# Two experts of the first batch move from the direct first stage to the Strassen-like slots of the second

## The chip, the cores and the metric

The program runs on one core of one Trainium2 chip, as one launch. The metric is the device time of the execution in microseconds (us). Beside it, a hardware profiler takes one execution apart into the instructions of each engine: TensorE (PE, with its weight loads as PEld), VectorE (DVE), ScalarE (ACT), GpSimd (POOL) and SyncE (SP), which here issues the DMAs. Each engine works through its own instructions strictly in the order written, and waits on semaphores for what other engines and DMAs produce.

## The reference, cut to what matters

```python
attn = clustered_attention(q, k, v, centroids)      # 4 batches, 8 heads, 768 rows, head size 64
x = attn.transpose(0, 2, 1, 3).reshape(3072, 512)
logits = x @ w_gate                                 # 8 experts
P = exp(logits - logits.max())
for _ in range(8):                                  # balanced over tokens and experts
    P /= P.sum(1, keepdims=True) + 1e-9
    P /= P.sum(0, keepdims=True) + 1e-9
    P *= N / E
for e in range(8):                                  # w1: 512 x 1024, w2: 1024 x 512
    out += P[:, e:e+1] * (relu(x @ w1[e]) @ w2[e])
```

All 3072 tokens go through all 8 experts.

## The kernel before, in words

The kernel has three parts one after the other: attention for all batches (to about 477 us of the span), a **first stage** that puts batch 0 through the 8 experts (to about 955 us), and a **second stage** that puts batches 1 to 3 through them (to the end). Every fp32 operand of a product is held as a sum of two fp16 halves, a high and a low one, and a product is three matmul passes (high by high, high by low, low by high).

**First layer, both stages.** `layer1` computes relu(x @ w1) for one quarter of an expert (256 of the 1024 hidden columns) with seven block products instead of eight (Strassen's method in Winograd's form). Each product is 6 matmuls of 384 columns (line 1387). It needs seven forms of the weights (three plain blocks and the sums S1 to S4) and seven of x. The results go through two PSUM banks in turn (`h_tile`): a quarter takes a bank for its first, second and fifth product, so that the first and the second product of a quarter can only begin when the sixth and the seventh of the quarter before have been read out by VectorE (`add`, line 1401).

**First stage.** The loop over t = 0 to 31 (lines 1582 to 1649) takes one quarter of an expert per turn of the loop, t = 4 * expert + quarter. In each of the seven products m of quarter t the program writes, in this order: the product and its read-out (`step(one)`), VectorE's low halves of relu results (`rests`), a piece of the magnitude scan for a later quarter (`scanning`), a piece of preparing x of batch 1 (`inputs`), a piece of making the weights for quarter t+1 (`making`), and one sixth of the second layer of quarter t-1 (`before`). This order is fixed on each engine by `plan.keep_order`. The second layer here is done directly: 36 matmuls of 512 columns per quarter (lines 1547 to 1549) into six PSUM banks, which collect over the four quarters of an expert. After an expert's last quarter VectorE multiplies the six banks by the gate and adds them to `acc` (lines 1560 and 1562), one per product of the following quarter.

Weights come raw from HBM (`load_raw`, 1 MB per quarter, 7 quarters ahead). ScalarE takes their magnitudes (`scan`, `total`, line 298), from which a power of two per expert is spread over all partitions by two small DMAs (`spread_powers`). `make_w` (lines 1507 to 1530) then makes the fp16 forms: ScalarE scales and makes high halves (1512, 1516, 1522, 1499), GpSimd the four sums and the low halves of w1's forms (332, 1517, 1524), VectorE the low halves of w2 (1502). `store_w` writes them to HBM, since the second stage uses them again. The forms of w1 live in a pool of three buffers (`wap`).

In quarters 1 to 3 the 8 rounds of balancing the gates (`gates`, lines 1289 to 1320) run on VectorE. Each round ends in a small matmul that rides in a product of those quarters (line 1315), the next round begins with its result.

**Second stage.** 24 slots, one per batch and expert. In slot n the first layer of (batch, expert) n runs with the second layer of slot n-1, 28 pairs of a first-layer product (6 matmuls of 384 columns) and a piece of the second layer (9 matmuls of 256 columns, line 1805). Here the second layer too is done with seven products, so it is 252 matmuls of 256 columns per expert. The hidden blocks are combined on GpSimd (`minus`, 1681), split by ScalarE and VectorE (1696, 1700), and the results are collected in four tiles C11, C21, C12, C22 and X by `evict` (1776, 1778). In the first eight slots the sums of w2 that this form needs are also made and stored (`second_sums`, `second_high`, `second_low`, lines 1706 to 1724).

The change touches the loop of the first stage, `load_raw`, `first_matrix`, `store_w`, `gated`, the pools at lines 1457 to 1465, the list of slots, `plan_slot`, `evict`, `layer1b` and `layer2b`.

Of the kernel before, what the change touches and what calls it, by code (L numbers as in the profile page):

```python
# [8 lines left out]
F32 = mybir.dt.float32  # L9
# [13 lines left out]
P = 128  # L23
# [141 lines left out]
def attn_moe_kernel(  # L165
# [138 lines left out]
    NP2 = NF // 2  # L304
    NI = E * NP2
# [977 lines left out]

    def h_tile():
        return ps_h.tile([P, 512], F32, name="h_ps")
# [36 lines left out]
    def spread_powers(am, n, name, use):  # L1322
# [4 lines left out]
        t = gs.tile([P, P, n], F32, name=f"all{n}", bufs=1)  # L1327
# [127 lines left out]
    before = iter(())  # L1455

    with ExitStack() as ax:
# [6 lines left out]
        accp = pool("accp", 1, ax)  # L1464
# [3 lines left out]
        def load_raw(idx):  # L1468
            e, f2 = divmod(idx, NP2)
            fs = slice(f2 * 2 * P, (f2 + 1) * 2 * P)  # L1470
            t = rawp.tile([P, 2048], F32, name="raw")
            nc.sync.dma_start(out=t[:, 0:1024].rearrange("p (c f) -> p c f", c=NC), in_=w1[e, :, fs].rearrange("(c p) f -> p c f", p=P))
            nc.sync.dma_start(out=t[:, 1024:2048].rearrange("p (j m) -> p j m", j=2), in_=w2[e, fs, :].rearrange("(j p) m -> p j m", p=P))
            raws[idx] = t
# [17 lines left out]
        def first_matrix(idx):  # L1492
            raw = raws[idx][:, 0:1024]
            return raw, raw.rearrange("p (k c t f) -> p t k c f", k=2, c=KC, t=2), sump.tile([P, 4, KC, P], F32, name="s1w")
# [37 lines left out]
        def store_w(idx, wt):  # L1532
            e, f2 = divmod(idx, NP2)
            wa, wb = wt
            if idx > 1:
                nc.sync.dma_start(out=w1d[idx], in_=wa.rearrange("p x a c f -> p (x a c f)"))
# [17 lines left out]
        def gated(e, acc):  # L1554
            gates_ = gate_values(0, e)

            def done(i, ps):
                gate = gates_[:, i : i + 1]
                if e == 0:
                    nc.vector.tensor_scalar(out=acc[:, i], in0=ps, scalar1=gate, scalar2=None, op0=ALU.mult)  # L1560
                else:
                    nc.vector.scalar_tensor_tensor(out=acc[:, i], in0=ps, scalar=gate, in1=acc[:, i], op0=ALU.mult, op1=ALU.add)
                if e == E - 1 and i % 2 == 1:
                    nc.scalar.dma_start(out=out_v[0][:, i - 1 : i + 1], in_=acc[:, i - 1 : i + 1])
# [3 lines left out]
        AHEAD = 7  # L1568
# [9 lines left out]
        acc = accp.tile([P, NT, DO], F32, name="acc")  # L1578
        scans = {i - 5: (i,) for i in range(8, NI)}
        loads = {0: (), 1: (4, 5), 2: (6, 7, 8), 3: (9, 10)}  # L1580
        loaded = {}
        for t in range(NI):
# [3 lines left out]
            for idx in loads.get(t, (t + AHEAD,) if t + AHEAD < NI else ()):  # L1586
                load_raw(idx)
            if 0 < t < NI - 1:
# [316 lines left out]
```

## Time and profile before

| | us |
|---|---|
| median of 3 runs | 2281.86 (2281.69 to 2282.4) |
| the profiled execution's own time | 2279.16 |
| its span, first to last instruction | 2277.1 |
| TensorE busy | 2236.1 (98%) |
| VectorE busy | 1649.1 (72%) |
| ScalarE busy | 1143.1 (50%) |
| GpSimd busy | 1118.1 (49%) |
| granted TensorE clock, mean | 0.995 |

The page in 40 slices of 57 us each (a digit is the busy share of a slice in tenths). The first stage is from the 9th to the 17th digit, the second stage follows:

```profile
PE   6999999999999999999999999999999999999999
DVE  7988878567666766588788877776676666666667
ACT  7777786555666665354444443333433333333333
POOL 3676787854555655276666653233332332322223
DMA  5345453365555543586766765544444554434433
```

Two things have to be kept in mind with such rows. Matmuls are pipelined, and one that shows 326 ns of duration follows the one before after about 163 ns, so the distance between starts is the measure. And the idle time of an engine that is not on the chain costs nothing.

### The profile page before, as it was taken

The numbers are of one execution on the slowest core, as the hardware profiler recorded it, in microseconds if no ns is written. First come the engines' busy times: TensorE is split into PE (matmuls) and PEld (weight loads), VectorE is DVE, ScalarE is ACT, GpSimd is POOL, SyncE is SP. The second block draws the span as 40 slices with busy tenths as digits, with TensorE's granted clock in tenths as the row PEclk, the third lists the DMA queues.
The fourth block names the chain that finished last, engine by engine and source line by source line (L and its number), as shares of the span: only waits on it lengthen the run. The fifth ranks groups of instructions, "written<-read, shape, count | busy, mean of one in ns | idle before, by whom it ended". The sixth has DMA issues, their size and how long they took to land.

```text
span 2277.1 us, 39662 instructions
## 1 busy us (share of the span) xinstructions
PE 2236.1 (98%) x15491; PEld 1458.8 (64%) x15491; DVE 1649.1 (72%) x2777; ACT 1143.1 (50%) x2107; POOL 1118.1 (49%) x997
## 2 busy tenths in 40 slices
PE   6999999999999999999999999999999999999999
PEld 3455554445555555567777777777777777777777
DVE  7988878567666766588788877776676666666667
ACT  7777786555666665354444443333433333333333
POOL 3676787854555655276666653233332332322223
PEclk7999999999999999999999999999999999999999
DMA  5345453365555543586766765544444554434433
GB/s 128 88 101 159 103 142 98 124 218 198 186 168 190 190 139 111 203 300 210 223 218 218 239 219 169 176 144 132 151 156 141 182 170 139 131 130 132 138 130 102
DMA packets 226860, 369.78 MB, mean 162 GB/s; under 512 B 73800, under 2 KB 163824, under 8 KB 226160
## 3 DMA queue, kind: packets, MB, share of 16 engines
q1 hardware_dynamic: 226240, 365.67, 50.3%
q8 instruction: 121, 1.98, 0.4%
q10 hardware_dynamic: 432, 1.57, 0.2%
q14 instruction: 67, 0.55, 0.1%
HBM read 272.22 MB, written 80.62 MB: 155 GB/s over the span
## 4 chain that ended last, share of the span: by engine, by line
PE 91%; DVE 6%; ACT 2%; issue 1%; DMA 1%; SPq 0%; DVEq 0%; ACTq 0%
PE h_ps L1387 38%; PE pb L1805 12%; PE pa L1805 8%; PE pc L1805 8%; PE av_ps L1004 4%; PE o_ps L1547 4%; PE o_ps L1549 4%; PE o_ps L1548 4%; PE exp_ps L945 2%; PE max_ps L849 2%; PE exp_ps L946 2%; DVE mrt L853 2%; PE misc_ps L1045 1%; PE misc_ps L630 1%; ACT pe L952 0%
## 5 line engine op out<-in xcount | busy, mean ns | idle before, releaser
L1387 PEld LDWEIGHTS <-wa 128*128 128x128 f16 x5376 | 525.6, 98 | 302.8 <-issue 5.3
L1805 PEld LDWEIGHTS <-ho 128*128 128x128 f16 x5940 | 580.8, 98 | 137.2 <-DVE ho L1700 1.1
L1387 PE MATMUL h_ps<-xsT,wa 128*128 128x384 f16 x3072 | 581.6, 326 | 1.2 <-DVE xsT L324 0.6
L1387 PE MATMUL h_ps<-xsB,wa 128*128 128x384 f16 x2304 | 436.9, 326 | 1.4 <-DVE B L1401 0.6
L1681 POOL TENSOR_TENSOR B<-B,B 128x768 f32<-128x768 f32 x96 | 197.9, 2064 | 468.2 <-DVE ho L1700 426.6
L1700 DVE TENSOR_TENSOR ho<-B,ho 128x768 f16<-128x768 f32 x283 | 348.1, 1230 | 1.6 <-ACT ho L1696 1.6
L1851 ACT ACTIVATE B<-B 128x384 f32<-128x384 f32 x288 | 149.7, 520 | 371.3 <-DVE B L1401 370.0
L1805 PE MATMUL pb<-w2o,ho 128*128 128x256 f16 x2532 | 322.2, 273 | 0.0
L1401 DVE SCALAR_TENSOR_TENSOR u<-h_ps,m 128x384 f32<-128x384 f32 x256 | 141.7, 553 | 243.5 <-PE h_ps L1387 240.7
L1696 ACT CAST ho<-B 128x768 f16<-128x768 f32 x283 | 226.8, 824 | 14.1 <-POOL B L1681 13.4
L970 POOL TENSOR_TENSOR psum<-psum,pe 128x512 f32<-128x512 f32 x160 | 208.1, 1317 | 43.6 <-ACT pe L952 40.3
L853 DVE TENSOR_REDUCE mrt<-max_ps 128x1 f32<-128x512 f32 (+1 forms) x288 | 188.8, 683 | 41.0 <-PE max_ps L849 39.7
L1805 PE MATMUL pc<-w2o,ho 128*128 128x256 f16 x1692 | 215.7, 273 | 0.3
L1805 PE MATMUL pa<-w2o,ho 128*128 128x256 f16 x1692 | 215.1, 273 | 0.0
L1681 POOL TENSOR_TENSOR B<-B,T 128x768 f32<-128x768 f32 x48 | 95.6, 1991 | 206.0 <-DVE ho L1700 206.0
L952 ACT ACTIVATE pe<-exp_ps 128x512 f32<-128x512 f32 x288 | 164.8, 597 | 56.9 <-PE exp_ps L946 51.2
L1411 ACT ACTIVATE m<-h_ps 128x384 f32<-128x384 f32 x128 | 62.6, 489 | 191.6 <-PE h_ps L1387 190.8
L1849 ACT ACTIVATE B<-h_ps 128x384 f32<-128x384 f32 x96 | 47.1, 490 | 211.4 <-PE h_ps L1387 211.4
L1549 PE MATMUL o_ps<-wb,hl 128*128 128x512 f16 x384 | 145.5, 379 | 0.0
L1548 PE MATMUL o_ps<-wb,hh 128*128 128x512 f16 x384 | 145.5, 379 | 0.0
L1547 PE MATMUL o_ps<-wb,hh 128*128 128x512 f16 x384 | 145.5, 379 | 0.0
L1610 ACT ACTIVATE hh<-c 128x384 f16<-128x384 f32 x128 | 66.9, 523 | 143.2 <-DVE c L1401 142.0
(281 smaller groups left out, 3280.8 us busy)
## 6 DMA issues: line engine op xcount, KB each, us to landing
wa<-w1d SPq DMA_DIRECT2D x98, 896.0 KB
w2o<-w2d SPq DMA_DIRECT2D x168, 512.0 KB
raw<-in_moe_w SPq DMA_DIRECT2D x60, 512.0 KB
w1d<-wa SPq DMA_DIRECT2D x30, 896.0 KB
r<-in_moe_w SPq DMA_DIRECT2D x32, 512.0 KB
w2d<-w2s SPq DMA_DIRECT2D x32, 512.0 KB
w2d<-wb SPq DMA_DIRECT2D x96, 128.0 KB
scan<-in_moe_w SPq DMA_DIRECT2D x32, 256.0 KB
```

The lines of the kernel that those rows point to most:

```text
L853: nc.vector.tensor_reduce(out=t["mr"][:, i0 : i0 + ni, ni - 1], in_=ps.rearrange("p (x c) -> p x c", x=ni), axis=AX, op=ALU.max)
L952: nc.scalar.activation(pe, ps.rearrange("p (x c) -> p x c", x=ni), AF.Exp, scale=SCALE)
L970: (nc.gpsimd if e == POOL else nc.vector).tensor_tensor(out=st[:, o : o + N0], in0=old[o], in1=part, op=ALU.add)
L1387: nc.tensor.matmul(ps[:, 0:HB], wa[:, w_, a, c, :], x[:, x_, c, :], start=(first and s_ == 0), stop=(s_ == len(steps) - 1), skip_group_che ...
L1547: nc.tensor.matmul(po[i], hh[:, t, ti], wbh[:, t], start=(first and t == 0), stop=False)
L1548: nc.tensor.matmul(po[i], hh[:, t, ti], wbl[:, t], start=False, stop=False)
L1549: nc.tensor.matmul(po[i], hl[:, t, ti], wbh[:, t], start=False, stop=(last and t == 1))
L1681: nc.gpsimd.tensor_tensor(out=t, in0=d[a], in1=d[c], op=ALU.subtract)
L1696: nc.scalar.copy(t[:, 0], blocks[n, g][o])
L1700: nc.vector.tensor_tensor(out=t[:, 1], in0=blocks[n, g][o], in1=t[:, 0], op=ALU.subtract)
L1805: nc.tensor.matmul(ps[q], h[:, h_, f, q * P : (q + 1) * P], w[:, 2 * g + f, w_], start=(first and g == 0 and s_ == 0 and q % 2 == 0), stop ...
L1851: rests.append(lambda: nc.scalar.activation(c, c, AF.Relu))
```

## The change

Experts 6 and 7 of batch 0 no longer go through the first stage. They become the first two slots of the second stage, which then has 26 slots; the loop of the first stage ends after 24 quarters (`NB`).

- Their weights were made by `make_w` in quarters 23 to 30. Now a generator `later` makes them during quarters 1 to 23, one turn per product (turn k falls in quarter 1 + k // 7, product k % 7 counted from 0). From turn 4 to turn 35 it takes the magnitudes of the 16 raw halves, one every second turn, alternately on ScalarE (`total`, w1) and on VectorE (`largest`, w2). From turn 36 a fixed list makes one quarter's weights every 13 turns, mostly one piece per turn. The raw halves are loaded twice, once for each purpose, into a pool of three half-size buffers.
- In that list the four sums are made on VectorE, where `make_w` has them on GpSimd. The low halves of the w1 forms stay on GpSimd.
- The fp16 forms use the same three buffers of `wap` as the quarters of the loop; they are stored to HBM by turn 16 of each quarter's list.
- Raw loads of the loop run 6 quarters ahead instead of 7, and the pool of raw tiles has 6 buffers instead of 8.
- The first stage's results are collected in the tiles C11, C21, C12, C22 of the second stage instead of `acc`: two evictions of 256 columns per bank instead of one of 512. X begins in the first slot. The output of batch 0 is written in the second slot, as that of the other batches in their last one.
- x of batch 1 is reloaded in the second slot instead of in the last quarter of the first stage.
- The w2 sums are made in the first eight slots of the new list, so for experts 6 and 7 first.

```diff
+    STD = E - 2
...
-        wbp = pool("wbp", 3, ax)
+        wbp = pool("wbp", 4, ax)
+        NB = STD * NP2
-        rawp = pool("rawp", 8, ax)
+        rawp = pool("rawp", 6, ax)
...
         def store_w(idx, wt):
+            if idx > 1:
+                store_first(idx, wt[0])
+            store_second(idx, wt[1])
...
             def done(i, ps):
                 gate = gates_[:, i : i + 1]
+                j, q = divmod(i, 3)
+                for r, name in enumerate((("C11", "C21"), ("C12", "C22"))[j]):
+                    o, y = totals[name][:, q], ps[:, r * HD : (r + 1) * HD]
+                    if e == 0:
+                        nc.vector.tensor_scalar(out=o, in0=y, scalar1=gate, scalar2=None, op0=ALU.mult)
+                    else:
+                        nc.vector.scalar_tensor_tensor(out=o, in0=y, scalar=gate, in1=o, op0=ALU.mult, op1=ALU.add)
...
-        AHEAD = 7
+        AHEAD = 6
...
+        def later():
+            whole = [(e, f2, m) for e in range(STD, E) for f2 in range(NP2) for m in range(2)]
+            todo, ahead, spreads = whole + whole, [], []
+            def fetch():
+                if todo:
+                    e, f2, m = todo.pop(0)
+                    t = rawp.tile([P, 1024], F32, name="rawx", bufs=3)
+                    fill_half(t, e, f2, m)
+                    ahead.append(t)
...
+            for _ in range(3):
+                fetch()
+            yield from wait(4)
+            for e in range(STD, E):
+                am = gs.tile([P, 2, NP2], F32, name="am8x")
+                for f2 in range(NP2):
+                    for m in range(2):
+                        t = ahead.pop(0)
+                        if m:
+                            largest(am[:, m, f2 : f2 + 1], t)
+                        else:
+                            total(am[:, m, f2 : f2 + 1], t, junkp.tile([P, 1024], F16, name="junk"))
+                        yield from wait(1)
+                        fetch()
+                        yield from wait(1)
+                am2 = gs.tile([P, 2], F32, name="am2x")
+                nc.vector.tensor_reduce(out=am2, in_=am, axis=AX, op=ALU.max)
+                spreads.append(spread_powers(am2, 2, f"amw{e}", lambda g, e=e: weight_use(e, g, gs), "x"))
...
+                return {
+                    0: [lambda: nc.scalar.activation(t1, t1, AF.Copy, scale=s1[:, e : e + 1])],
+                    2: [lambda: summed(0, 1)],
+                    3: [second_high],
+                    4: [lambda: summed(2, 3)],
+                    5: [plain_high],
+                    6: [lambda: second_low(0)],
+                    7: [lambda: plain_low(0)],
+                    8: [lambda: second_low(1), lambda: nc.scalar.copy(into["wa"][:, 0, 3:7], S_)],
+                    9: [lambda: plain_low(1)],
+                    11: [lambda: sum_low(0), fetch],
+                    12: [lambda: store_second(idx, into["wb"])],
+                    13: [lambda: sum_low(2), fetch],
+                    16: [lambda: store_first(idx, into["wa"])],
+                }
+            TURN = 13
...
+        extra = later()
-        for t in range(NI):
+        for t in range(NB):
...
                 if m:
                     step(making)
+                if t > 0:
+                    step(extra)
                 if m:
                     step(before)
                 if m == 1:
                     store_w(t, wt)
-                if t == NI - 1:
-                    reload_x(1, RIGHT[m])
...
-    slots = [(b, e) for b in range(1, B) for e in range(E)]
+    slots = [(0, e) for e in range(STD, E)] + [(b, e) for b in range(1, B) for e in range(E)]
...
-        if b == 1:
+        if n < E:
```

## Rows read from the trace of the kernel before

**Rows 1.** The page's first part: busy us, share of span, instructions

```profile
PE 2236.1 (98%) x15491; PEld 1458.8 (64%) x15491; DVE 1649.1 (72%) x2777; ACT 1143.1 (50%) x2107; POOL 1118.1 (49%) x997
```

**Rows 2.** The page's chain that ended last, shares of the span by line

```profile
PE h_ps L1387 38%; PE pb L1805 12%; PE pa L1805 8%; PE pc L1805 8%; PE av_ps L1004 4%; PE o_ps L1547 4%; PE o_ps L1549 4%; PE o_ps L1548 4%; PE exp_ps L945 2%; PE max_ps L849 2%; PE exp_ps L946 2%; DVE mrt L853 2%; PE misc_ps L1045 1%; PE misc_ps L630 1%; ACT pe L952 0%
```

**Rows 3.** Chain in order of time, first stage: start us, us, what

```profile
903.64 1.95 PE h_ps L1387 x12
918.24 1.95 PE h_ps L1387 x12
```

**Rows 4.** The same view, one slot of the second stage apart

```profile
1697.32 0.97 PE h_ps L1387 x6
...
1752.13 0.97 PE h_ps L1387 x6
```

**Rows 5.** The same view, start of the first stage

```profile
512.01 0.51 DVE csum L1312
512.56 0.39 PE h_ps L1315 x2
```

**Rows 6.** VectorE's timeline there: start us, us, instruction, idle before

```profile
508.10 0.75 DVE L1502 SCALAR_TENSOR_TENSOR wb<-raw,s,wb 128x512 f16<-128x512 f32 x1
509.09 0.17 DVE L1318 TENSOR_SCALAR csum<-h_ps 128x8 f32<-128x8 f32 x1 [0.25 <-ACT m L1411]
523.31 0.55 DVE L1401 SCALAR_TENSOR_TENSOR c<-h_ps,u 128x384 f32<-128x384 f32 x1
535.24 0.56 DVE L1401 SCALAR_TENSOR_TENSOR c<-h_ps,m 128x384 f32<-128x384 f32 x1 [0.99 <-PE h_ps L1387]
```

**Rows 7.** TensorE at the second product of two quarters, timeline

```profile
524.43 1.14 PE L1387 MATMUL h_ps<-xsT,wa 128*128 128x384 f16 x6
...
729.32 1.14 PE L1387 MATMUL h_ps<-xsT,wa 128*128 128x384 f16 x6
```

**Rows 8.** Timeline of VectorE, quarter after an expert's end

```profile
726.33 1.64 DVE L1502 SCALAR_TENSOR_TENSOR wb<-raw,s,wb 128x512 f16<-128x512 f32 x1
727.89 0.74 DVE L1562 SCALAR_TENSOR_TENSOR acc<-o_ps,gates,acc 128x512 f32<-128x512 f32 x1
728.55 0.54 DVE L1401 SCALAR_TENSOR_TENSOR c<-h_ps,u 128x384 f32<-128x384 f32 x1
```

**Rows 9.** Stretches: us; busy PE, PEld, DVE, ACT, POOL; clock; DMA share, GB/s

```profile
510.00:520.00 10.00, 9.24 (x52) 4.88 (x51) 9.36 (x24) 4.43 (x8) 5.14 (x7) 1.00 1.07 385
713.80:728.40 14.60, 14.60 (x80) 7.64 (x79) 11.72 (x18) 9.81 (x16) 8.09 (x8) 1.00 0.56 191
```

**Rows 10.** VectorE's reductions to one column by line: ns min/median/max

```profile
L301 DVE TENSOR_REDUCE am<-xqB x12: 936/944/949, 609.6 to 1483.1; 128x1 f32<-128x768 f32 x12
L301 DVE TENSOR_REDUCE amx<-xT x1: 3333/3333/3333, 178.8 to 178.8; 128x1 f32<-128x3072 f32 x1
```

**Rows 11.** VectorE's only sums of line 332, 128 wide

```profile
L332 DVE TENSOR_TENSOR tx<-tx x4: 271/282/293, 303.5 to 444.5; 128x128 f32<-128x128 f32 x4
```

**Rows 12.** Groups by line of the whole span: an eviction of the second stage

```profile
L1778 DVE SCALAR_TENSOR_TENSOR C<-pb,gates,C 128x256 f32<-128x256 f32 x204 | 86.0, 476 | 19.4 <-PE pb L1805 19.4
```

**Rows 13.** Groups by line, ACT, steady first stage: busy us, mean ns

```profile
L298 ACT ACTIVATE junk<-raw 128x1024 f16<-128x1024 f32 x46 | 48.0, 1044 | 0.0
L1512 ACT ACTIVATE raw<-raw,s 128x1024 f32<-128x1024 f32 x27 | 30.8, 1139 | 10.0 <-DVE s L267 10.0
L1522 ACT CAST wa<-s1w 128x1024 f16<-128x1024 f32 x27 | 27.8, 1028 | 0.0
```

**Rows 14.** Groups by line, POOL, the same stretch

```profile
L1524 POOL TENSOR_TENSOR wa<-s1w,wa 128x512 f16<-128x512 f32 x54 | 70.3, 1323 | 53.2 <-ACT wa L1522 53.2
L1517 POOL TENSOR_TENSOR wa<-raw,wa 128x512 f16<-128x512 f32 x27 | 36.9, 1367 | 0.0
```

**Rows 15.** SyncE's waits in the first stage: total us, times, longest

```profile
SPq L1328 <- DMA amw<-am: 15.0, 6, 2.9
```

**Rows 16.** The chain in order of time, start of the second stage

```profile
983.12 2.24 DVE ho L1700
```

More of the change, by code (lines that the diff above doesn't have):

```diff
@@ L1320, in gates, with spread_powers @@
             nc.vector.tensor_tensor(out=pr, in0=pr, in1=c2.unsqueeze(1).broadcast_to([P, NTT, E]), op=ALU.mult)
-    def spread_powers(am, n, name, use):
+    def spread_powers(am, n, name, use, own=""):
         d = dram.tile([P, n], F32, name=name)
@@ L1326, in spread_powers @@
         yield
-        t = gs.tile([P, P, n], F32, name=f"all{n}", bufs=1)
+        t = gs.tile([P, P, n], F32, name=f"all{n}{own}", bufs=1)
         nc.sync.dma_start(out=t, in_=d.partition_broadcast(P))
@@ L1455, in attn_moe_kernel, with total_tile @@
     before = iter(())
+    totals = {}
+    def total_tile(name):
+        return accp.tile([P, 3, HD], F32, name=name, bufs=2 if name == "C21" else 1)
     with ExitStack() as ax:
@@ L1493, in first_matrix @@
             raw = raws[idx][:, 0:1024]
-            return raw, raw.rearrange("p (k c t f) -> p t k c f", k=2, c=KC, t=2), sump.tile([P, 4, KC, P], F32, name="s1w")
+            return raw, raw.rearrange("p (k c t f) -> p t k c f", k=2, c=KC, t=2), sump.tile([P, 4, KC, P], F32, name="s1w" if idx < NB else "s1x")
         def second_matrix(idx, wb):
@@ L1581, in attn_moe_kernel, with enumerate_quarter @@
+        def enumerate_quarter(i, idx, turn):
+            return [(i * turn + y * 1, (i, y)) for y in (0, 2, 3, 4, 5, 6, 7, 8, 9, 11, 12, 13, 16)]
+        extra = later()
+        for name in ("C11", "C21", "C12", "C22"):
+            totals[name] = total_tile(name)
+        loads = {0: (), 1: (4, 5), 2: (6, 7, 8), 3: (9,)}
         loaded = {}
-        for t in range(NI):
+        for t in range(NB):
             e, f2 = divmod(t, NP2)
@@ L1585, in attn_moe_kernel @@
                 po = []
-            for idx in loads.get(t, (t + AHEAD,) if t + AHEAD < NI else ()):
+            for idx in loads.get(t, (t + AHEAD,) if t + AHEAD < NB else ()):
                 load_raw(idx)
-            if 0 < t < NI - 1:
+            if 0 < t < NB - 1:
                 wts[t + 1] = w_tiles()
                 making = make_w(t + 1, wts[t + 1])
-            if t + 2 >= NI:
+            if t + 2 >= NB:
                 loaded[t + 2] = load_wa((t + 2) % NI)
@@ L1648, in attn_moe_kernel @@
             wts.pop(t - 1, None)
-            before = layer2(po, hh, hl, wt, f2 == 0, f2 == NP2 - 1, gated(e, acc) if f2 == NP2 - 1 else None)
-        for x in (sink, inputs, scanning):
+            before = layer2(po, hh, hl, wt, f2 == 0, f2 == NP2 - 1, gated(e) if f2 == NP2 - 1 else None)
+        for x in (sink, inputs, scanning, extra):
             for _ in x:
@@ L1773, in evict @@
                 t, gate = totals[name][:, q], gates_[:, 3 * j + q : 3 * j + q + 1]
-                if e == 0 and (name, q) not in begun:
+                if (e == 0 or n == 0 and name == "X") and (name, q) not in begun:
                     begun.add((name, q))
@@ L1797, in layer2b @@
                 if name not in totals:
-                    totals[name] = accp.tile([P, 3, HD], F32, name=name, bufs=2 if name == "C21" else 1)
+                    totals[name] = total_tile(name)
             count = 0
```

92 lines of the change are left out of this document (68 added, 24 removed).

## The prediction

> **What bounds the kernel now.** I read the busy shares first: TensorE is at work for 98% of the span, the next engine for 72% [rows 1]. The chain that ended last confirms it: nearly all its shares are TensorE lines, 38% of them the first layer's [rows 2]. So a change pays by taking matmul time away, and loses where another engine makes TensorE wait. Then I looked for the pace in both stages. In the chain, the pair of products that begins a quarter of the first stage starts at 903.64 and again at 918.24, so a quarter takes 14.60 us [rows 3], and an expert 4 x 14.60 = 58.40. In the second stage the same place of a slot comes 54.81 us later [rows 4]. All quarters from the fifth on and nearly all slots keep these paces, so there is hardly a wait in either to be won. The third reading is the exception, the start of the first stage: there the chain runs through VectorE. TensorE waits for the end of a round of the gates (512.01 + 0.51, matmul at 512.56) [rows 5], and VectorE is busy 9.36 of 10 us in that stretch [rows 9].
>
> **What the change removes and adds on TensorE.** Two experts leave the first stage (2 x 58.40 = 116.80) and come back as two slots (2 x 54.81 = 109.62): 7.18 us less. Nothing else changes on TensorE's own list. The slots in which w2's sums are made are still eight, so the two new ones are slots without this work.
>
> **What it adds elsewhere.** The weights of the eight late quarters were made in the eight quarters that are now gone; they are made now beside 23 others. I go through the engines by what TensorE would wait for.
>
> *VectorE, magnitudes.* Eight reductions of 1024 columns. The trace has 768 columns in 0.944 us and 3072 in 3.333 [rows 10], so (3.333 - 0.944) / 2304 = 1.037 ns a column, and 1024 take 1.21 us. They come at turns 6, 10, 14, 18 (quarters 1 to 3, the stretch where VectorE has no room) and 22, 26, 30, 34.
> - Turn 6 stands behind the low half that ends at 508.10 + 0.75 = 508.85; the next round of the gates begins at 509.09 after 0.25 us of idle time [rows 6]. Of 1.21 us, 0.96 push the round, and TensorE already waits for its end: +0.96.
> - Turn 10 pushes the last read-out of quarter 2 from 523.31 to 524.52, with its 0.55 to 525.07 [rows 6]. That read-out frees the bank of the next quarter's second product, which starts at 524.43 [rows 7]: +0.7 with the hand-over.
> - Turns 14 and 18 stand among the last rounds. The first idle time behind them is 0.99 at 535.24 [rows 6]; of 2.42 us some 1.4 are left and a part falls into quarter 4: I take +1.2.
> - Turn 26 falls into the sixth product of quarter 4, where expert 0 is evicted. The pattern is that of quarter 16: low half, eviction, then the last read-out at 728.55 to 729.09 [rows 8], and the bank is wanted at 729.32 [rows 7]. Only 0.23 us are free, so of 1.21 us about 1.0, with the longer eviction ahead (below) 1.2. Turns 22, 30 and 34 fall where VectorE waits for TensorE anyway: nothing.
>
> Together 0.96 + 0.7 + 1.2 + 1.2 = 4.1. The ends: 0.96 if only the first is felt, five times 1.21 = 6.1 if all five are felt in full.
>
> *VectorE, evictions.* A bank took one eviction of 0.74 [rows 8], it takes two of 256 columns now, 0.476 each by the second stage's row [rows 12]: 0.21 more per bank. Five of six have TensorE's end of the bank behind them, the one ahead of the last read-out uses up the 0.23 us of slack named above. I take nothing for it alone; if that slack is less than it looks, 5 x 0.21 = 1.05.
>
> *VectorE, sums and low halves.* Each quarter of the list has four sums and two low halves. The sums on VectorE are not in this trace at 256 columns: at 128 they take 0.282 [rows 11], so up to 0.56 by twice that, and at least 0.28. A low half is the same instruction as in `make_w`, 0.75 alone and 1.64 beside GpSimd [rows 6, 8]. In a quarter with evictions VectorE is busy 11.72 of 14.60 us [rows 9]; 2.2 us come on top in the mean (2 x 0.56 a turn twice, and 2 x 1.2, in 13 turns of 2.1 us, makes 4.6 per 27 us). It fits, but the slack is not everywhere. In quarters 8, 12 and 16 such a pair or half falls into the fifth product, just ahead of the tight place of [rows 8]. The idle time there takes most of it: I take 0.4 each, 1.2 in all; between 0 and 3 x 1.64 = 4.9. In other quarters the last read-out has no evictions ahead, nothing.
>
> *ScalarE.* Magnitudes 1.04, scaling 1.14, high halves about 1.03 to 1.14 by the same rows [rows 13], one piece a turn of 2.1 us. ScalarE is busy 9.81 of 14.60 us in a full quarter [rows 9] and some 2 us come on top; it has most of a product to spare before TensorE needs the bank that it reads. Nothing; if the cover is gone it is the second rival.
>
> *GpSimd.* Two low pieces of 1.32, one of 1.37 and one of about half of that per 13 turns [rows 14], on an engine that is busy 8.09 of 14.60 [rows 9]: nothing for itself. But it does its work beside VectorE. The row shows what that costs VectorE: the low half 1.64 instead of 0.75 [rows 6, 8]. The Trainium skill, SBUF — State Buffer, "Who interferes with whom", says why: a VectorE instruction with two SBUF inputs and a GpSimd instruction that reads SBUF exclude each other, and the later one waits for the whole of the other; the two rows agree with it. What this could make of the time stands under the third rival.
>
> *DMA and SP.* 16 MB of halves are read (twice 8 MB), where 8 MB were read raw. At the start the queues run at 385 GB/s with a share of 1.07, so they are full [rows 9]. Three halves of 0.5 MB ahead of the loads cost 1.6 MB / 385 = 4 us of queue, and each half is fetched five turns (over 10 us) before use: I take nothing. Upper end: one such wait of 4 us.
>
> *Border of the stages.* The start of the second stage keeps its waits on VectorE, 2.24 us on the chain [rows 16], with less DMA beside it, since x is reloaded a slot later. Nothing; between -2.24 and, at the new border of batches, +2.24.
>
> **Sum.** -7.18 + 4.1 + 1.2 = -1.9 us. The profiled execution took 2279.16 us, so 2277.3 by its own time; the median of the runs is 2.7 above it, and the same difference makes 2281.86 - 1.9 = **2280.0**. What the measurement can tell from no change is 0.2%, 4.6 us.
>
> **Rivals.**
>
> 1. *VectorE recovers.* If its backlog at the start is worked off in the gaps, only turn 6 is felt, and -7.18 + 0.96 = -6.2: 2275.7. For it: TensorE waits for VectorE only where a bank or a round is due, and the fixed list puts single pieces between. Against it: the row of 9.36 in 10 us, and the 0.23 us of slack.
>
> 2. *The third weight buffer is the wait (slower).* The list takes its fp16 tile at its turn 5 from the same three buffers as the loop. With two tiles of the loop in between, it gets the buffer of the list's quarter before, whose store is issued at that quarter's turn 16, two turns (4.3 us) before ScalarE wants to write. The store is 0.9 MB: 2.4 us at 385 GB/s, and a small DMA on this queue is waited for 2.9 us at the longest [rows 15], so 5.3 us. When SP issues the store no earlier than its turn, ScalarE stands for a microsecond seven times and more where SP is held up, and behind it stand the read-outs that TensorE needs. With 1.2 us each reaching TensorE: 7 x 1.2 = 8.4 on top of -1.9, +6.5: 2288.4. It decides from 0.95 us each. Against it: SP may issue as soon as GpSimd's last low piece is done, at turn 14.
>
> 3. *VectorE and GpSimd block each other.* The list moves pieces to both. If in each of the 16 quarters with the list (turns 36 to 143, quarters 6 to 21) half of the 0.89 us (1.64 - 0.75) reaches the last read-out: 16 x 0.45 = 7.2 on top, +5.3: 2287.2. The rule of the skill named above would work in this way. Against it: GpSimd and VectorE overlap in every quarter now, and no quarter from the fifth on loses anything.
>
> 4. *The gain isn't there:* a slot at the head of the second stage could be slower than 54.81. The rows of both kinds of slots speak against it.
>
> **How the numbers follow.** The forecast has 0.52, rival 1 0.26, rivals 2 and 3 together 0.20, rival 4 0.02 with no gain left. The unknown costs alone reach from 7.18 - 0.96 = 6.2 below (8.5 if the border's 2.24 go as well) to 6.1 + 1.05 + 4.9 - 7.18 = 4.9 above, with one DMA wait 8.9 above. I take 2275.6 to 2287.0; what lies above is the worse half of rivals 2 and 3. By the 4.6 us: faster 0.26, no change 0.54, slower 0.20. The forecast's own range is 2277.5 to 2284.
>
> **What would show it.** Quarters of 14.60 us and slots of 54.81 with 26 of them: the gain. First stage: quarters 1 to 4 longer by 3 to 5 us together, with TensorE waiting on VectorE (rounds and read-outs), and quarters 9, 13 and 17 beginning with a wait of a few tenths. If ScalarE's first copy into the list's tile waits for a DMA, rival 2 is at work; if quarters without evictions grow too while VectorE's low halves take 1.6 us throughout, rival 3. I am wrong if quarters 1 to 4 keep their length, or if the waits come from a queue that I priced at nothing.

## The result, and the profile after

The changed kernel took 2307.76 us (median of 4 runs, 2304.91 to 2310.28) against 2282.13 for the kernel before on the same chip: ratio 1.011 with a 95% interval of 1.0094 to 1.0126. It is 25.6 us slower. Forecast were 2280.0, in a range up to 2287.0: the prediction was wrong. Each profile is of one execution: that of the kernel before took 2279.16 us, that of the changed kernel 2304.91.

The page of the changed kernel, its busy shares and the shares of the chain that ended last:

```profile
span 2303.1 us, 40251 instructions
...
PE 2239.4 (97%) x15707; PEld 1481.5 (64%) x15707; DVE 1706.7 (74%) x2885; ACT 1148.2 (50%) x2111; POOL 1137.2 (49%) x983
...
PE 80%; DVE 10%; DMA 4%; ACT 2%; POOL 2%; issue 1%; SPq 1%; DVEq 0%; ACTq 0%; POOLq 0%
```

The last of these lines in the page of the kernel before:

```profile
PE 91%; DVE 6%; ACT 2%; issue 1%; DMA 1%; SPq 0%; DVEq 0%; ACTq 0%
```

TensorE's share of the chain fell from 91% to 80%; VectorE, DMAs and GpSimd took its place. Where that is shows in the length of each quarter, which I take from the start of a quarter's first product to that of the next (every 42nd matmul of line 1387, after the change 1390). Quarters 0 to 22, in us. (The last quarter of the loop, 31 before and 23 after, takes 22.4 us both times: it holds the border of the stages, 7.8 us.)

| quarters | before | after |
|---|---|---|
| 0 to 3 | 14.65 15.33 16.04 15.29 | 16.07 15.34 16.87 16.84 |
| 4 to 7 | 14.60 each | 21.62 14.60 17.62 16.52 |
| 8 to 11 | 14.60 each | 14.60 16.54 14.60 17.12 |
| 12 to 15 | 14.60 each | 16.57 15.39 14.91 16.00 |
| 16 to 22 | 14.60 each | 16.74 15.26 15.71 15.82 16.23 14.74 14.60 |

The sum closes. From the last quarter's end to the end of the span the second stage takes 1431.6 us instead of 1322.1: 109.5 more, which is two slots of 54.8 [rows 4]. Eight quarters of 14.60 are gone (116.8), so 7.3 us are won. The 24 quarters left, the border among them, are 31.7 longer than the same ones before, and the stage begins 1.6 later: -7.3 + 31.7 + 1.6 = 26.0, the difference of the spans.

The largest single loss is quarter 4. The chain of the changed kernel, start and length in us:

```profile
545.66 4.84 DMA amw<-am2x
550.51 5.16 DMA all2x<-amw
555.69 0.43 DVE gmax L1335
...
557.87 0.48 DVE u L1404
558.39 2.08 PE h_ps L1390 x6
```

These are the two small DMAs that spread the magnitude of expert 6. The list put the reduction of `all2x` three turns (6.3 us) behind `am2x`; the DMAs took 10 us, and VectorE, which works in order, stood at the reduction. Behind it stood the evictions and the read-out `u` that TensorE needs. In VectorE's timeline (idle time before, and what ended it, in brackets):

```profile
555.69 0.42 DVE L1335 TENSOR_REDUCE gmax<-all2x 128x2 f32<-128x256 f32 x1 [6.79 <-DMA all2x<-amw]
...
557.01 0.87 DVE L1584 TENSOR_SCALAR C<-o_ps,gates 128x256 f32<-128x256 f32 x2
557.79 0.55 DVE L1404 SCALAR_TENSOR_TENSOR u<-h_ps,m 128x384 f32<-128x384 f32 x1
```

And such a stop costs twice. The engines' busy time, the granted clock of TensorE (PEclk) and the DMA share in stretches around this stop and the one of expert 7:

```profile
core 0: us, PE busy (x) PEld busy (x) DVE busy (x) ACT busy (x) POOL busy (x), PEclk, DMA share, GB/s
546.00:557.00 11.00, 8.21 (x43) 4.05 (x42) 3.93 (x12) 7.37 (x14) 4.57 (x6) 1.00 0.68 233
557.00:564.00 7.00, 5.61 (x17) 2.38 (x17) 7.00 (x14) 1.88 (x3) 2.38 (x2) 0.51 0.63 218
...
594.00:598.00 4.00, 1.14 (x7) 0.44 (x6) 1.96 (x9) 0.19 (x1) 0.49 (x1) 1.00 0.14 20
598.00:601.40 3.40, 3.06 (x11) 1.35 (x10) 3.40 (x8) 1.66 (x5) 0.00 (x0) 0.50 0.51 39
```

At the two stops 4.56 and 3.24 us lie between the starts of two matmuls. Behind them TensorE was granted the lower of its two levels, 1.2 instead of 2.4 GHz, for 6.8 and for 3.4 us.

The waits of quarters 0 to 23, us in total, times, longest; the first and the third are what TensorE felt of VectorE, the last is rival 2's:

```profile
PE h_ps L1390 <- DVE c L1404: 12.9, 14, 2.9
DVE gmax L1335 <- DMA all2x<-amw: 12.0, 2, 6.8
...
PE h_ps L1390 <- DVE u L1404: 8.5, 5, 4.2
ACT wa L1665 <- DMA w1d<-wa: 7.4, 3, 3.6
```

And the DMA queue's own waits. SP stands at the raw load until VectorE has freed the buffer, which it never does in the kernel before, and it now waits up to 7.7 us for a small DMA of the loop where 2.9 was the longest [rows 15].

```profile
SPq L1489 <- DVE wb L1518: 58.9, 14, 9.9
SPq L1331 <- DMA amw<-am: 20.5, 4, 7.7
```

### The profile page after: what moved, and what is told of

The parts are those of the page before. It is cut to its first block, busy times and chain, and to the rows that moved or that the text cites. A ratio compares the mean times of both kernels' runs of the same rounds, so it can differ in the third digit from the quotient of the medians.

```text
span 2303.1 us, 40251 instructions
## 1 busy us (share of the span) xinstructions
PE 2239.4 (97%) x15707; PEld 1481.5 (64%) x15707; DVE 1706.7 (74%) x2885; ACT 1148.2 (50%) x2111; POOL 1137.2 (49%) x983
## 4 chain that ended last, share of the span: by engine, by line
PE 80%; DVE 10%; DMA 4%; ACT 2%; POOL 2%; issue 1%; SPq 1%; DVEq 0%; ACTq 0%; POOLq 0%
PE h_ps L1390 32%; PE pb L1934 13%; PE pa L1934 9%; PE pc L1934 9%; PE av_ps L1005 5%; PE exp_ps L946 2%; PE max_ps L850 2%; PE exp_ps L947 2%; DVE mrt L854 2%; DVE wb L1518 1%; PE o_ps L1570 1%; PE o_ps L1569 1%; PE o_ps L1568 1%; DVE hl L1744 1%; PE misc_ps L1046 1%
## 5 line engine op out<-in xcount | busy, mean ns | idle before, releaser
L1934 PEld LDWEIGHTS <-ho 128*128 128x128 f16 x6444 | 630.3, 98 | 148.5 <-DVE ho L1830 0.8
L1830 DVE TENSOR_TENSOR ho<-B,ho 128x768 f16<-128x768 f32 x307 | 374.8, 1221 | 4.2 <-ACT ho L1826 4.2
L1934 PE MATMUL pb<-w2o,ho 128*128 128x256 f16 x2748 | 349.7, 273 | 0.0
L1826 ACT CAST ho<-B 128x768 f16<-128x768 f32 x307 | 246.0, 824 | 17.3 <-POOL B L1811 16.6
L1934 PE MATMUL pc<-w2o,ho 128*128 128x256 f16 x1836 | 233.8, 273 | 0.3
L1934 PE MATMUL pa<-w2o,ho 128*128 128x256 f16 x1836 | 233.4, 273 | 0.0
L1404 DVE SCALAR_TENSOR_TENSOR B<-h_ps,u 128x384 f32<-128x384 f32 x208 | 114.8, 552 | 49.7 <-PE h_ps L1390 48.9
L1005 PE MATMUL av_ps<-pe,vn 128*64 128x512 f32 (+1 forms) x768 | 134.4, 492 | 0.0
L947 PE MATMUL exp_ps<-qX 98*128 98x256 f16 (+1 forms) x384 | 119.9, 327 | 0.4 <-DMA qX<-mt 0.4
L850 PE MATMUL max_ps<-qX 96*128 96x256 f16 (+1 forms) x384 | 103.7, 335 | 11.8 <-DVE mrt L854 8.6
```

Source lines behind the costliest of these rows:

```text
L947: nc.tensor.matmul(o, t["k2"][0:98, ki], t["qa"][0:98, a:z], start=False, stop=True)
L1005: nc.tensor.matmul(av[o, a:z], vn[:, i, :], heads[t]["pe", c][:, i - i0], start=(i == 0), stop=False, skip_group_check=True)
L1404: nc.vector.scalar_tensor_tensor(out=t, in0=ps[:, 0:HB], scalar=KAPPA, in1=x, op0=ALU.mult, op1=ALU.add)
L1826: nc.scalar.copy(t[:, 0], blocks[n, g][o])
L1830: nc.vector.tensor_tensor(out=t[:, 1], in0=blocks[n, g][o], in1=t[:, 0], op=ALU.subtract)
L1934: nc.tensor.matmul(ps[q], h[:, h_, f, q * P : (q + 1) * P], w[:, 2 * g + f, w_], start=(first and g == 0 and s_ == 0 and q % 2 == 0), stop ...
```

## The experiments

"Excess" below is what the 24 quarters of a run take over 24 x 14.60 and the usual 7.8 at the border; it is 34.5 in the changed kernel and 2.9 in the first 24 of the kernel before. Quarter 0 varies by up to 2.2 us with a spell at the lower clock (3.4 us, in e9 6.8) that most runs have near 486 and the profiled run of before had not. Later quarters that an edit does not touch repeat closely (quarter 13: 15.39, 15.38, 15.38, 15.39 in the changed kernel, e2, e3 and e4), so single quarters say more than whole times. The letters in the expectations hold within their own group of runs. A time without an interval is from a single run.

**e1: the move alone.** `later` is empty; the two slots use the weights of experts 0 and 1.

```diff
-        nc.sync.dma_start(out=wa.rearrange("p x a c f -> p (x a c f)"), in_=w1d[idx])
+        nc.sync.dma_start(out=wa.rearrange("p x a c f -> p (x a c f)"), in_=w1d[idx % (STD * NP2)])
...
-        extra = later()
+        extra = iter(())
```

> The move without the making: 24 quarters, 26 slots, but nothing is made for experts 6 and 7 of batch 0 in the first stage; their two slots use the stored weights of experts 0 and 1 (so the values of these slots are not the reference's; matmuls, loads and stores of the second stage are the same in number and size). Theory A (the loss is what the list puts into the first stage): the whole gain shows, 7.2 us less than before, 2275 us, with quarters of 14.60 and slots of 54.81. Rival B (the gain was never there, because the new border or the slots cost more): 2280 or above, with the excess in the second stage.

2275.43 us, ratio 0.9971 (0.9961 to 0.998), as theory A said; its ten runs lie between 2271.5 and 2280.5. All quarters from the fifth on are 14.60 but one (14.97). So the gain of 7 us is there, and evictions, the smaller raw pool and the border cost nothing. All the loss is in `later`.

**e2: the spreads' steps three turns apart.**

```diff
-                    for s in spreads:
-                        step(s)
+                    if turn[0] % 3 == 2:
+                        for s in spreads:
+                            step(s)
+                    turn[0] += 1
```

> As the changed kernel, but each step of spreading the two late experts' magnitudes comes three turns after the one before, so VectorE reaches the reduction 9 turns (19 us) after the first small DMA instead of 3 (6.3 us). Theory A1 (VectorE, in order, stands at the reduction for two small DMAs that take some 10 us together, and TensorE's clock falls behind the longer stops): quarters 4 and 6 lose 7.0 and 3.0 us in the changed kernel, both go to under 2, the time falls by 7 to 9 us, to about 2297 to 2299. Rival C (the loss lies in the 16 halves and the list as such): less than 3 us.

2298.99. Quarter 4 falls from 21.62 to 14.60 and quarter 6 from 17.62 to 14.60, which shows the mechanism. But quarter 8 goes from 14.60 to 19.28 and quarter 5 to 15.67, and the excess is still 28.3 (the expectations round it up to 28.4). So the time lies where A1 had it, but of the 10.0 us of the two quarters only 6.2 are won on the whole.

**e3 and e4: no second loading of the halves**, in the changed kernel and in e2.

```diff
-                    t = rawp.tile([P, 1024], F32, name="rawx", bufs=3)
-                    fill_half(t, e, f2, m)
-                    ahead.append(t)
+                    if len(kept) < 3:
+                        t = rawp.tile([P, 1024], F32, name="rawx", bufs=3)
+                        fill_half(t, e, f2, m)
+                        kept.append(t)
+                    ahead.append(kept[(32 - len(todo) - 1) % 3])
```

> As the changed kernel, but only the first three raw halves are loaded, and all later uses take these three tiles again (and the list's first scaling multiplies by 1), so 29 of the 32 loads of 0.5 MB are gone, with values that are not the reference's. Rival D (the loads fill the DMA queues, and all the waits follow from that): nearly the whole loss of 33 us goes, about 2278. Theory A: the spreading gets shorter by the queue's share, and waits for stores go, but VectorE's own pieces ahead of tight read-outs stay: about 10 to 15 us are won, 2292 to 2297.

2300.74, outside what D and A gave: quarter 4 is 18.82, quarter 6 15.50. The small DMAs of expert 6 take 3.38 and 4.81 us in place of 4.84 and 5.16, those of expert 7 5.42 and 4.56 in place of 8.51 and 3.73. The other quarters do not shrink together: 9 is 1.0 shorter, 16 is 1.7 longer. The miss is mine: the loads are a part of what stands ahead of the spread, not of the rest.

> Both of the earlier cuts at once: the spreading three turns a step, and only three raw halves loaded (values not the reference's). What is left of the loss then comes neither from the spreading nor from the extra loads. Theory A (two halves: small or late DMAs whose landing an engine stands for, and VectorE's and GpSimd's own pieces ahead of tight read-outs): about 12 to 15 us over the move alone remain, spread over quarters 6 to 20 with 0.3 to 2 us each, so 2288 to 2292. Rival D (DMA alone): 2280 or less.

2299.6, a miss of both theories: without the loads the excess is 27.1, e2 has 28.3. Quarter 8 (19.05) shows in VectorE's timeline, and in GpSimd's below it, what its late reduction met:

```profile
605.60 0.41 DVE L1335 TENSOR_REDUCE gmax<-all2x 128x2 f32<-128x256 f32 x1
606.04 0.68 DVE L1336 TENSOR_SCALAR gmax<-gmax 128x2 f32<-128x2 f32 x1
606.75 1.07 DVE L1337 TENSOR_SCALAR gmax<-gmax 128x2 int32<-128x2 int32 x1
607.87 1.08 DVE L266 TENSOR_SCALAR ginv<-gmax 128x2 f32<-128x2 f32 x1
...
609.23 0.55 DVE L1404 SCALAR_TENSOR_TENSOR c<-h_ps,u 128x384 f32<-128x384 f32 x1
```

```profile
603.65 3.04 POOL L1540 TENSOR_TENSOR wa<-s1w,wa 128x512 f16<-128x512 f32 x2
606.66 2.26 POOL L1679 TENSOR_TENSOR wa<-s1x,wa 128x512 f16<-128x512 f32 x2
```

Operations on two values, 0.17 us each elsewhere, take 0.68, 1.07 and 1.08 while GpSimd works without a pause on the loop's and the list's low pieces, and the read-out `c` stands behind them. TensorE stands for it (2.9 us between two matmuls) and then has 3.4 us at the lower clock.

**e5: the list's sums back on GpSimd**, in e2.

```diff
-                    sums(S_, A[:, 1, 0], A[:, 1, 1], A[:, 0, 0], A[:, 0, 1], nc.vector, which)
+                    sums(S_, A[:, 1, 0], A[:, 1, 1], A[:, 0, 0], A[:, 0, 1], nc.gpsimd, which)
```

> As the run with late spreads (2299.0), but the list's four sums are on GpSimd instead of VectorE. Theory A (VectorE's sums stand ahead of its read-outs and wait for GpSimd): quarters 9 to 20 get shorter, 4 to 8 us less, 2291 to 2295. Rival E (it is the list's low halves and GpSimd's load; with the sums on it GpSimd is late with the loop's weights): the same or slower, 2299 or more.

2297.14: quarters 12, 16, 18 and 20 get shorter by 1.1 to 1.8, quarters 8, 15, 17 and 21 by 0.7 to 1.4 longer. The loss moves with the pieces. Neither expectation is met.

**e6, e7, e8: the traffic alone.** In e1, the loads of the halves are issued at the list's turns (e6), or at the turns of the list's stores the loop's current weights are stored (e7), or both (e8). e7 and e8:

```diff
+                    if f == "load":
+                        more()
+                    elif f == "second":
+                        store_second(idx, now[0][1])
+                    else:
+                        store_first(idx, now[0][0])
```

> The move alone (2275.4) with the 32 loads of raw halves put back at the list's turns, and nothing read of them. Theory A: the loads alone cost little, at most 3 us more than the move alone, 2275 to 2279. Rival D (the loads fill the queues and delay the loop's own spreading and loads): at least 8 us more, 2283 or above.

> The two experts are moved, nothing is made or loaded for them (the kernel of e1), but at the turns of the list at which its weights are stored, the loop's current weights are stored in their place (0.9 MB and 0.39 MB, eight times), to rows that nobody reads. Theory Q (the queue: bulk transfers stand ahead of the loop's own small ones): one or two of the loop's spreads in quarters 11, 15 and 19 come late and the first stage is 3 to 6 us longer than in e1: 2278.5 to 2281.5 us. Theory R (the engines: VectorE's and GpSimd's pieces ahead of the read-outs): stores alone cost no more than the loads alone did (1.1 us): 2275 to 2277.

> As e7, with the 32 loads of halves as well: all the late quarters' DMA traffic, none of their work on the other engines. Q: the traffic adds up and the loop's spreads land 7 us and more after their issue: 6 to 12 us over e1, 2281.5 to 2287.5. R: at most 2 us over e1, 2275 to 2277.5.

2276.48, 2278.65 and 2281.91: 1.1, 3.2 and 6.5 over e1, e6 as A and e7 and e8 as Q said. The first two lie within the spread of e1's ten runs, so the quarters have to decide. By quarters from the second on it is 1.7 for the loads (quarter 9), 4.4 for the stores (quarter 15) and 7.6 for both (quarters 7, 9, 11, 15). The chain of e8, in which SP issues the DMAs and no other engine does a stroke for the late experts:

```profile
578.37 6.99 DMA amw<-am
...
607.15 8.41 DMA xqB<-xd
...
639.29 6.54 DMA amw<-am
...
698.13 8.86 DMA amw<-am
707.05 4.45 DMA all<-amw
```

These are the loop's own small DMAs (and one of x). Nothing reads e8's halves, so their loads need not wait for a reader as in the changed kernel: the turns are the same, the moments of issue are not quite. Ahead of the small DMA in quarter 15, in e7, the raw load (1 MB) and two stores of w1's forms (0.9 MB each) had been issued in the 7 us before.

**e9: e2 without the list's stores.**

```diff
-                    12: [lambda: store_second(idx, into["wb"])],
...
-                    16: [lambda: store_first(idx, into["wa"])],
```

> The kernel of e2 (the changed kernel with the late experts' spreads taken three turns apart) without the stores of the late experts' weights; their slots use the weights of experts 0 and 1. Everything else is made as before. Q: ScalarE no longer waits for a store and the loop's spreads land early; of e2's 28 us over the even pace 7 to 12 go: 2287 to 2292. R: 1 to 3 go: 2296 to 2298.

2298.38, excess 28.8, 0.4 above R's range and 6 above Q's: quarters 15, 16 and 8 are 1.2, 0.6 and 1.4 shorter than in e2, quarter 7 is 1.6 longer and quarter 9 2.0. So the waits for stores are a loss of some quarters, not the body of it.

**e10 and e11: e9 without GpSimd's pieces of the list, and without VectorE's.**

```diff
# e10
-                    7: [lambda: plain_low(0)],
-                    9: [lambda: plain_low(1)],
-                    11: [lambda: sum_low(0), fetch],
+                    11: [fetch],
-                    13: [lambda: sum_low(2), fetch],
+                    13: [fetch],
# e11
-                    2: [lambda: summed(0, 1)],
-                    4: [lambda: summed(2, 3)],
-                    6: [lambda: second_low(0)],
```

> The kernel of e9 (late spreads, no stores, weights of experts 0 and 1 in the two slots) without the list's four pieces on GpSimd; ScalarE's and VectorE's pieces stay. Theory B (VectorE and GpSimd block each other): of e9's 28.9 us over the even pace 8 to 14 go: 2284 to 2290. Theory V (VectorE's own pieces stand ahead of the read-outs, whoever works beside it): at most 4 go: 2294 to 2298.

> The kernel of e9 without the list's four sums and two low halves on VectorE; the copies of ScalarE and the low pieces of GpSimd read the raw half in place of the sums. V: 12 to 18 us go: 2280 to 2286. B: without its partner GpSimd still meets the loop's own low halves on VectorE, 4 to 9 go: 2289 to 2294.

2289.64 and 2290.25. In quarters 12 to 22 (the list is under way, no late spread is left) e9 loses 9.7 us, e10 1.5, e11 0.6. Either half of the pieces alone is nearly free. A stretch of 165 or 164 us of these quarters in e9, e10 and e11 in turn: busy us (and instructions) of PE, PEld, DVE, ACT, POOL, then PEclk, DMA share, GB/s.

```profile
670.00:835.00 165.00, 157.19 (x832) 81.14 (x831) 135.17 (x217) 111.51 (x178) 120.24 (x113) 1.00 0.54 177
```

```profile
668.00:832.00 164.00, 163.17 (x870) 84.92 (x869) 128.18 (x223) 115.17 (x183) 95.08 (x94) 1.00 0.55 181
```

```profile
668.00:832.00 164.00, 163.75 (x874) 85.40 (x873) 119.59 (x192) 115.62 (x184) 121.58 (x117) 1.00 0.55 180
```

VectorE is busy 82%, 78% and 73% of them, GpSimd 73%, 58% and 74%. With both lists on them TensorE stands for 7.8 us, with one of them for 0.8 and 0.3. Both times lie in B's ranges and outside V's. That the two must come together is shown by this; why they do (blocking or the sum of both loads) is not. What is left of their excess is mostly in quarters 7 to 11 (7.9 and 10.5 us), where small DMAs are late: `xqB` 8.42 us in quarter 9 of e10, `amw` 7.85 in quarter 11 of e11.

**e12: 14 turns instead of 13**, in e2.

```diff
-            TURN = 13
+            TURN = 14
```

> The kernel of e2 with one size changed: a late quarter every 14 turns instead of 13, so that each piece always meets the same product of the loop. If the drift through all products is what hits the tight read-outs (and the order of the pieces is good where it begins), of the 28.4 us over the even pace 10 to 15 go: 2284 to 2289. If each late quarter has its price wherever it begins, 2296 to 2301.

2309.7, excess 39.3: above both. The theory of the drift, on which v1 rested, falls: in quarters 16 to 22, where the list's loss stands alone, 5.8 us are lost (e2 6.9), now all in every second quarter (17, 19, 21: 16.46, 15.94, 17.22). So a late quarter has its price in this order of pieces. The rest is the queue again: in the chain x of batch 1 takes 7.15 us and `amw` of the loop 9.29 and 10.48, and quarters 9, 11 and 15 are 19.01, 18.58 and 22.12.

**v1 to v4: versions with all the work.** v1 is e2 with 14 turns, the list begun 4 turns later, magnitudes on ScalarE alone and the pieces put at other turns, VectorE's into the first four products of a quarter, behind its tight read-outs. v2 begins the list 7 turns later, keeps the late spreads away from quarters with a spread of the loop and reloads w1 for the border later. v3 loads two halves behind expert 2's spread instead of ahead of it. v4 has the list's low pieces on VectorE and stores the w1 forms a turn earlier. The core of v1's and v3's edits:

```diff
# v1
-                    2: [lambda: summed(0, 1)],
-                    3: [second_high],
+                    1: [plain_high],
+                    2: [lambda: plain_low(0), lambda: plain_low(1)],
+                    3: [lambda: summed(0, 1)],
                     4: [lambda: summed(2, 3)],
...
-                    8: [lambda: second_low(1), lambda: nc.scalar.copy(into["wa"][:, 0, 3:7], S_)],
...
+                    7: [lambda: nc.scalar.copy(into["wa"][:, 0, 3:7], S_)],
...
# v3
-            yield from wait(11)
+            yield from wait(7)
+            fetch()
+            yield from wait(2)
+            fetch()
+            yield from wait(2)
```

> The changed kernel rearranged: spreading as in the run with late spreads, all magnitudes on ScalarE, and the list repeated every 14 turns instead of 13 (two whole quarters), so that each piece stays in the same product: VectorE's sums in the second and third product of one quarter, its low halves in those of the next, ScalarE's pieces in the sixth and seventh, GpSimd's in the seventh and first; the store is issued 4 turns before its buffer is written again instead of 2. Theory A: nearly all of the loss goes, 2275 to 2279, a little below before. Rival D (DMA load): the loads are all there, so most of the loss stays, over 2295.

2299.61, ratio 1.0074 (1.0058 to 1.0091): a miss of theory A by 20 us, and in the range of D, which blamed the DMA load. From quarter 16 on nearly all quarters are 14.60, so the engines are cured there, but quarters 11, 13 and 15 take 20.8 to 21.6. The chain names the queue:

```profile
642.80 7.89 DMA amw<-am
650.75 5.24 DMA all<-amw
...
677.93 11.86 DMA w1d<-wa
```

> The rearranged kernel once more. It lost 6 to 7 us each in quarters 11, 13 and 15, where the loop's or the list's engines stood for DMAs: the loop's spreading was queued behind the list's 0.9 MB store and a raw half, and a store landed 12 us after its issue. Now the list begins one quarter later, so that its stores fall into the quarters in which the loop spreads nothing, its first load comes in the seventh product instead of the fourth, and the late experts' spreading keeps out of the quarters in which the loop spreads. The first two loads of weights for the second stage come in its last quarter. Theory A: these three stops go, 2275 to 2281. Rival D: the stops move elsewhere, over 2290.

2285.87, ratio 1.0018 (1.0008 to 1.0028): 14 us better than v1, some 5 over the expectation of A. One quarter is left with such a stop: quarter 7, 18.44, `amw` 7.45 and `all` 4.79 us. Its 3.84 us of loss are a stop (2.38 us between two matmuls) and the lower clock behind it.

> v2 with two of the first three halves for the list loaded 4 and 6 turns later, behind the spread of expert 2 instead of ahead of it. Q: the wait of 3.84 us in quarter 7 and the halved clock behind it go, the other quarters stay as in v2: 2281 to 2283 us, level with the kernel before. R: quarter 7 keeps more than 2 us of it: 2284 to 2286.

2283.06, ratio 1.0001 (0.9991 to 1.001): the time that Q gave, and quarter 7 is 14.60. But the other quarters did not stay as Q had it, so that the number fits is in part luck: the profiled runs of v2 and v3 took 2282.97 and 2282.93 us, with an excess of 12.1 and 12.4. Now x of batch 1 comes late in quarter 9, and ScalarE waits for a store.

```profile
606.67 8.34 DMA xqB<-xd
...
686.23 9.38 DMA w1d<-wa
```

> v3 with the list's four low pieces on VectorE instead of GpSimd, in turns that fall behind VectorE's tight read-outs, and the store of the w1 forms issued a turn earlier. Theory B (the list's loss in quarters 11 to 22 needs both engines at work on it): quarters 11 to 22 together no more than 2 us over the even pace (v3: 4.9 and a wait for a store), 2278 to 2281 us, level with or a little ahead of the kernel before. Theory V (VectorE's own time ahead of the read-outs): the pieces that VectorE gets on top make it worse, 2284 to 2288.

2281.21, ratio 0.9998 (0.9989 to 1.0007), 0.2 above B's range. Quarters 11 to 22 lose 3.6 us (v3 4.8), more than the 2 that B allowed: 0.4 to 1.1 in five of them. So VectorE's longer list seems to have a price too, about as large as what GpSimd's absence saves; v4 changed a store as well, so this is argued and not shown. No version beats the kernel before by more than the measurement can tell.

## Why the prediction was wrong, step by step

*The gain* was right: 7.18 forecast, 7.3 in the trace, 7.0 in e1. Rival 4 is refuted, and so are costs of the evictions, the border and the shorter lead of the raw loads by itself: e1 has them all.

*Magnitudes on VectorE.* For the quarters of the gates 0.96 + 0.7 + 1.2 = 2.9 were forecast; quarters 2 and 3 lose 0.8 and 1.5, together 2.4. Right. The 1.2 for turn 26 can't be seen behind the stop of quarter 4, but e2 has it as 1.1 in quarter 5, whose second product waits for the read-out that the magnitude pushes:

```profile
558.32 1.21 DVE L301 TENSOR_REDUCE am8x<-rawx 128x1 f32<-128x1024 f32 x1
559.45 0.86 DVE L1584 TENSOR_SCALAR C<-o_ps,gates 128x256 f32<-128x256 f32 x2
560.23 0.54 DVE L1404 SCALAR_TENSOR_TENSOR c<-h_ps,u 128x384 f32<-128x384 f32 x1
```

***DMA and SP: "I take nothing".* This is the step that failed.** It priced bandwidth and the lead of the halves, and passed over the two small DMAs of each late expert, which it did not even list, though the list reduces their result three turns later. Their price, with a halved clock after each: 7.0 us in quarter 4 and 3.0 in quarter 6, which e2 takes away. A wait of 2.9 us [rows 15] was taken for the most that such a DMA costs (rival 2). But each of these six waits has a pause of 4 us or more in the queue ahead of it: at 634.24, for one, the last store had been issued 6.4 us earlier, and the last large one 9 us. Among the loads and stores of the list the four DMAs took 3.7 to 8.5 us. SP's timeline of the kernel before shows that gap:

```profile
627.84 0.50 SPq L1538 DMA_DIRECT2D w2d<-wb  x1
634.24 0.33 SPq L1325 DMA_DIRECT2D amw<-am  x1
637.15 0.33 SPq L1328 DMA_DIRECT2D all<-amw  x1
```

The same queue makes the loop's own small DMAs late: 7.6 us by e8 without any work on the engines. Most of that is not the changed kernel's own loss (4.6 of the 7.6 lie in quarter 15, which loses 1.4 there), but it shows that the queue alone can make TensorE wait. My upper end for all of this was one wait of 4 us, and the range, which ends at 2287.0, left out even that.

*GpSimd "nothing for itself"; VectorE "it fits".* Each was right alone: e10 and e11 lose 1.5 and 0.6 us in quarters 12 to 22. Together they lose 9.7, so this is the second step that failed. This is rival 3 in kind, over a stretch of 11 quarters; it was forecast at 7.2 over 16. It had its chance together with rival 2 (0.20) and should have been more than a rival. "It fits" was also added up wrongly: 4.6 us per 27 are 2.5 per quarter and not 2.2, which on top of 11.72 leaves 0.4 of 14.60. That a blocked instruction by itself is what TensorE waits for is not shown: in e11 VectorE's low halves of `hl` are as long as in e9 or longer (911 ns in the mean, 820 in e9) and TensorE hardly waits. My reading is that it takes longer pieces and no idle time left behind them; no run tests that by itself.

The operations on 128x2 values that took 1.07 us in e4 were not in my sum at all. The Trainium skill, SBUF — State Buffer, "Who interferes with whom", has them too: a one-input VectorE operation in a 2-port mode and GpSimd exclude each other, and by its page VectorE: DVE Perf Modes, "Mode 2×_2P", such a mode is for single-source operations between SBUF operands. The run agrees: 0.17 us alone, 1.07 and 1.08 beside GpSimd. I had cited this rule for two-input instructions only.

*ScalarE "nothing"; rival 2.* The wait is there (7.4 us in three times; two stores of w1's forms, 7.61 and 7.10 us, stand on the chain), but e9, without it, is 0.6 us faster. Its mechanism was right, its price was not (nor its threshold: 4.6 and 1.9 over seven make 0.93 and not 0.95). ScalarE's magnitudes are not free either: in v1 to v4, which have all of them there, quarter 2 still is 0.6 longer than in e1.

*What adds up and what doesn't.* By its own quarters the changed kernel loses 1.4 in quarter 0 (chance, see above), 2.4 in 2 and 3 (magnitudes), 10.0 in 4 and 6 (the late spreads), 6.4 in 7 to 11 and 11.4 in 12 to 22: 31.6 of 31.7. For 12 to 22 e9 still has 9.7, and either half of the pieces alone 1.5 or less. The parts are not independent: e2 took 10 away and got 6 back in quarters 5 and 8 (1.1 of it the magnitude of turn 26, which the stop had hidden), and e9 took the stores away and lost elsewhere what it won. How the queue's and the engines' shares split in quarters 7 to 11 of the changed kernel stays open.

## What to carry to other kernels

A small DMA whose result an in-order engine needs can cost what is queued ahead of it, so list what the queue was given just before, and put the instruction that waits for it where nothing urgent stands behind. Two engines that each have room for the added work need not have room for it together: look at both busy shares in the tight stretch, and try each half alone. Taking spare buffers away can be free until something else is added to the queue. In e1, with the smaller raw pool and nothing of the list, SP already stands at the raw loads and waits up to 5.4 us for a small DMA, at no loss:

```profile
SPq L1492 <- DVE wb L1521: 124.2, 15, 12.2
SPq L1331 <- DMA amw<-am: 14.1, 4, 5.4
```

That the eight buffers of before would have kept the loads apart from the stores in the changed kernel is likely from this, but no run gave them back.

## What the runs showed of the hardware that was not expected

- The stops of TensorE in quarters 4 and 6 (4.56 and 3.24 us between two matmuls) were followed by 6.8 and 3.4 us at a granted clock of 0.5, with matmuls of 384 columns 320 ns apart instead of 163. So a stop of 4.56 us made quarter 4 longer by 7.0.
- VectorE operations on 128x2 values took 0.17 us as a rule and up to 1.08 beside GpSimd; the same operations on 128x1 values took 0.15 beside it (both e4, 606.04 to 608.95 and 701.68).
- A store of 0.9 MB landed 11.86 us after its issue in v1 (issued at 677.93), while 151 GB/s were moved at a DMA share of 1.03 (680 to 690 us); at the start of the stage 385 GB/s went through at 1.07 [rows 9].
